# Masks and softmax sums as column-tiled products, and a transpose buffer moved to another PSUM pool, in a recurrent attention kernel

## The chip, the cores and the metric

The kernel runs on one core of a Trainium2 chip. The metric is the device time of one launch in microseconds (us), as the median of several launches.

The engines are named as the profile names them: PE is TensorE's matrix products, PEld its loads of the stationary operand, DVE is VectorE, ACT is ScalarE, POOL is GpSimd. An *eviction* is the copy of a product's result from its PSUM buffer to the buffer that later work reads. A *turn* is VectorE's transpose of a projection in 32x32 blocks (`STREAM_TRANSPOSE`); a cast follows it.

## The reference, cut to what matters

Four layers run one after the other: A, B, A, B. Layer A is a segmented attention that this change doesn't touch. Layer B is recurrent: 64 segments of 32 tokens, each with 8 memory rows in front, and the memory of a segment is the output of the one before. So the 64 steps are a chain, and nothing of one step's queries can start before the last step's output.

```
def _B_ref(x, mem0, Wq, Wk, Wv, Wo, seg_len):      # D = 640, H = 32 heads, Dh = 128, M = 8
    mem = mem0
    for s in range(n_seg):                         # 64 steps
        h = jnp.concatenate([mem, xs], axis=1)     # 40 rows
        q, k, v = (einsum('btd,dhe->bhte', h, W) for W in (Wq, Wk, Wv))
        scores = einsum('bhqe,bhke->bhqk', q, k) * scale
        scores = where(mask, scores, -1e9)
        p = softmax(scores)
        o = einsum('bhte,hed->btd', einsum('bhqk,bhke->bhqe', p, v), Wo)
        mem = o[:, :M, :]
    ...
x = x + _A_ref(_layernorm(x), ...); x = x + _B_ref(_layernorm(x), ...)   # and both once more
```

## The kernel before

A step of layer B works on two halves of 16 heads, b = 0 and 1. Its projections are *column-tiled*: four products with 32 stationary columns each sit side by side in the 128x128 array and write to the four groups of 32 partitions (`tile_position=(0, 32 * j)`), which the profile shows as `128*32`. Scores and output projection have this form too (half of the score products use only 8 of the 32 columns). The mask (an identity times the mask, which starts the accumulation that the scores add to) and the sums (a block matrix of ones times the exponentials) are whole products, `128*128`. The products with the values are row-tiled, `32*128`.

```
def ln_tr(g):                                     # transposes of the layer norm, in the last step of each four
    xn = ln_n.pop(g)
    tps = ps_tile([128, NCH, 128], BF16, "b_lntps")         # pool of 3 PSUM banks, shared with all that follows
    for c in range(NCH):
        nc.tensor.transpose(tps[:, c, :], xn[:, 128 * c:128 * c + 128], C.identb[:])
    ...
def scores(b):
    t = SP[b] = ps_tile([128, 512], F32, "b_SP")
    ...                                            # sp is a view of the first 224 columns of t
    nc.tensor.matmul(sp[:, :, 0:40], lhsT=C.identb[:], rhs=mask..., start=True, stop=False)
    for r in range(4):
        for k, n in ((0, 32), (1, 8)):
            for j in range(4):
                nc.tensor.matmul(o, lhsT=KT..., rhs=QT..., start=False, stop=True, tile_position=(0, 32 * j))
    nc.scalar.activation(out=PT[:, b]..., in_=t[:, 0:224], func=ACT.Exp, ...)

def sums(b):
    ...                                            # 4 products, lhsT = blk[:, k] (128 x 128)

def normalise(b):
    nc.scalar.activation(out=flat, in_=SP[b][:, 256:480], func=ACT.Ln)
    nc.scalar.activation(out=flat, in_=flat, func=ACT.Exp, scale=-1.0)
    nc.vector.tensor_tensor(out=PT[:, b], in0=PT[:, b], in1=R[:], op=ALU.mult)
    ...
# the middle of a step; each qk() is 20 products and a 32x32 turn plus a cast on VectorE
qk(W.wq, "b_Qa", 0, QT); qk(W.wk, "b_Ka", 0, KT)
while late: late.pop(0)()                          # residual add of the last step, 2 x 0.5 us on VectorE
...
qk(W.wq, "b_Qb", 1, QT)
scores(0)
qk(W.wk, "b_Kb", 1, KT)
while xn_pending: ln_tr(xn_pending.pop(0))         # one step in four
sums(0); normalise(0)
VPass(0).run()                                     # 20 products, then evac("dve", Vsb[:, 0, :], ...)
scores(1)
V1 = VPass(1); V1.run(3)
values(0)                                          # the row-tiled products: need PT (normalised) and Vsb
...
V1.run(2)
sums(1)
take("act", 0, 0); take("act", 0, 1)               # evictions of the values, on ScalarE
normalise(1)
...
op.run(4); op.run(4)                               # output projection of the first half
...
```

In the traces each engine starts its work in program order (only TensorE's loads run ahead of its products). The four steps of each group differ a little. I call them kinds 0 to 3: in kinds 0, 1 and 3 the last step's residual add sits between the turns of Ka and Qb on VectorE, kind 2 is without it, and kind 3 has the layer norm's transposes.

## Time and profile before

| | kernel before |
|---|---|
| time | 2560.89 us median of 3 (2560.43 to 2561.15) |
| PE busy | 2346.4 us, 92% of the profiled span of 2552.9 us |
| DVE busy | 1668.9 us, 65% |
| a step of layer B, median of kinds 0, 1, 2, 3 | 13.81, 13.83, 13.94, 14.70 us |

A step is measured in the trace from its first Q product to the next step's. Two layers have 64 steps each; the medians are over the 30 to 32 steps of one kind.

The windows view of the kernel before, one line for most of the first layer B: span, busy time (and count) of PE, PEld, DVE, ACT, POOL, then granted clock, DMA share, GB/s:

```profile
370.00:1252.00 882.00, 862.95 (x23072) 470.08 (x23068) 600.54 (x1289) 250.04 (x737) 372.31 (x842) 1.00 0.09 22
```

PE is busy for 863 of 882 us there, at full clock. It is tempting to read this as "TensorE is the limit, and whatever shortens its work shortens the time". The Trainium skill, "Perfetto Trace Analysis", section "Identifying the Most-Contended Engine", warns that busy time of matmuls is no good measure of how near TensorE is to its limit, because they are pipelined. Here is TensorE in a step of kind 0 (start us, duration us, engine, operation, out<-in, shape, count):

```profile
819.85 1.27 PE L91 MATMUL b_Qb<-b_wq,b_hT 128*32 128x512 bf16 x20
821.04 0.24 PE L91 MATMUL b_SP<-b_mask,c_identb 128*128 128x160 bf16 x1
821.27 0.37 PE L91 MATMUL b_SP<-b_QT,b_KT 128*32 128x40 bf16 x32
821.48 1.28 PE L91 MATMUL b_Kb<-b_wk,b_hT 128*32 128x512 bf16 x20
822.70 0.33 PE L91 MATMUL b_SP<-b_PT,b_blk 128*128 128x160 bf16 x4
822.96 1.26 PE L91 MATMUL b_V<-b_wv,b_hT 128*32 128x512 bf16 x20
824.15 0.24 PE L91 MATMUL b_SP<-b_mask,c_identb 128*128 128x160 bf16 x1
824.33 0.37 PE L91 MATMUL b_SP<-b_QT,b_KT 128*32 128x40 bf16 x32
824.55 0.84 PE L91 MATMUL b_V<-b_wv,b_hT 128*32 128x512 bf16 x12
825.32 0.20 PE L91 MATMUL b_OTL<-b_PT,b_Vsb 32*128 32x40 bf16 x4
```

Read the starts, not the durations: a group's duration runs to the modelled end of its last product, and the next group starts before that. From Qb to the first mask are 1.19 us, though two projections in a row are 1.08 us apart; mask to scores takes 0.18 us or more.

VectorE in the same stretch of the kernel before:

```profile
820.15 0.72 DVE L91 STREAM_TRANSPOSE b_TQ<-b_Ka 128x512 f32<-128x512 f32 x1
820.90 0.23 DVE L91 CAST b_KT<-b_TQ 128x128 bf16<-128x128 f32 x1
821.05 1.00 DVE L91 TENSOR_TENSOR b_XO<-b_OPS,b_XO 64x320 f32<-64x320 f32 x2
822.08 0.72 DVE L91 STREAM_TRANSPOSE b_TQ<-b_Qb 128x512 f32<-128x512 f32 x1
...
823.94 0.61 DVE L91 TENSOR_TENSOR b_PT<-b_PT,b_R 128x224 bf16<-128x224 bf16 x1
824.47 0.68 DVE L91 CAST b_Vsb<-b_V 128x512 bf16<-128x512 f32 x1
```

VectorE works without a pause from the turn of Ka to the eviction of V at 825.15 (824.47 + 0.68), and TensorE's value products start at 825.32. An engine that is busy for 65% of the span has no slack in this half of the step, and TensorE comes only 0.17 us after it.

The transposes of a step of kind 3, TensorE before; the bracket is the idle time before a group and what ended it:

```profile
806.78 1.28 PE L91 MATMUL b_Kb<-b_wk,b_hT 128*32 128x512 bf16 x20
808.14 0.44 PE L91 MATMUL b_lntps<-c_identb,b_xn 128*128 128x128 bf16 x5
808.42 0.32 PE L91 MATMUL b_SP<-b_PT,b_blk 128*128 128x160 bf16 x4
809.03 1.26 PE L91 MATMUL b_V<-b_wv,b_hT 128*32 128x512 bf16 x20 [0.29 <-DVE b_TQ L91]
```

The transposes take a turn in the pool of three banks, so they wait for VectorE's turn of Qb, and V then waits for that of Kb.

### The profile page before, as it was taken

What the parts mean: (1) busy time and instruction counts of PE and PEld (TensorE: products, weight loads), DVE (VectorE), ACT (ScalarE), POOL (GpSimd) and SP (SyncE); (2) the same over time, 40 slices, a digit from 0 to 9 for tenths busy, and PEclk for the clock granted to TensorE, in tenths of its full rate; (3) what the DMA queues carried; (4) which work ended last, traced back from release to release, by engine and by line L of the source; (5) the groups of instructions that cost most, each with busy time, mean ns of one, the idle gap of its engine ahead of it and who ended that gap; (6) DMA issues with size and microseconds to landing.
All of it is one profiled execution on the core that took longest, in us unless ns stands there. A gap on an engine that the chain in (4) does not pass through costs nothing. (4 is left out here: it accounts for less than half of the span.)

```text
span 2552.9 us, 119988 instructions
## 1 busy us (share of the span) xinstructions
PE 2346.4 (92%) x53196; PEld 1266.5 (50%) x53196; DVE 1668.9 (65%) x3771; ACT 921.6 (36%) x2067; POOL 1014.8 (40%) x2333
## 2 busy tenths in 40 slices
PE   6888979999999999999778879699999999999997
PEld 3444435555555555555434445355555555555554
DVE  5666646676666666766556666466766766676665
ACT  4666722222323232222256657132222222222322
POOL 2334434444444444444323334244444444444442
PEclk9988979999999999999989889899999999999999
DMA  6563340001000110000123233400000000000000
GB/s 184 145 173 96 104 133 22 22 22 24 23 22 23 24 23 23 24 20 19 36 88 109 78 105 110 138 20 20 21 20 19 20 19 21 20 19 22 17 16 15
DMA packets 98834, 131.62 MB, mean 52 GB/s; under 512 B 20592, under 2 KB 84096, under 8 KB 96384
## 3 DMA queue, kind: packets, MB, share of 16 engines
q1 hardware_dynamic: 96704, 122.20, 17.4%
q8 instruction: 418, 6.85, 1.1%
q10 hardware_dynamic: 1600, 1.66, 0.2%
q14 instruction: 112, 0.92, 0.1%
HBM read 89.17 MB, written 26.21 MB: 45 GB/s over the span
## 5 line engine op out<-in xcount | busy, mean ns | idle before, releaser
L91 PEld LDWEIGHTS <-b_hT 128*32 128x32 bf16 x15520 | 418.9, 96 | 332.0 <-issue 46.0
L91 ACT ACTIVATE b_PT<-b_SP 128x224 bf16<-128x224 f32 x256 | 91.4, 357 | 871.9 <-PE b_SP L91 871.9
L91 PE MATMUL b_V<-b_wv,b_hT 128*32 128x512 bf16 x5120 | 348.4, 382 | 8.1 <-DVE b_TQ L91 8.1
L91 ACT ACTIVATE a_PT<-a_S 128x768 bf16<-128x768 f32 (+1 forms) x384 | 325.3, 892 | 78.3 <-PE a_S L91 72.7
L91 PE MATMUL b_OPS<-b_wo,b_OTsb 128*32 128x320 bf16 x8192 | 325.3, 300 | 5.4 <-DVE b_OTsb L91 5.3
L91 POOL TENSOR_TENSOR b_Rtot<-b_Rtot,b_R 128x160 bf16<-128x160 bf16 x256 | 158.2, 618 | 306.0 <-ACT b_R L91 306.0
L91 POOL CAST b_QT<-b_TQ 128x384 bf16<-128x384 f32 x254 | 140.7, 554 | 328.8 <-DVE b_TQ L91 328.8
L91 DVE CAST b_Vsb<-b_V 128x512 bf16<-128x512 f32 x256 | 175.7, 686 | 119.7 <-PE b_V L91 119.6
L91 PEld LDWEIGHTS <-b_OTsb 128*32 128x32 bf16 x8192 | 195.9, 96 | 100.6 <-DVE b_OTsb L91 50.2
L91 ACT CAST b_OTsb<-b_OTL 128x320 bf16<-128x320 f32 x384 | 150.9, 427 | 226.3 <-PE b_OTL L91 192.0
L91 POOL CAST b_KT<-b_TQ 128x384 bf16<-128x384 f32 x254 | 142.6, 562 | 130.4 <-DVE b_TQ L91 130.4
L91 POOL TENSOR_SCALAR_AFFINE_SELECT a_PT<-a_PT 128x256 bf16<-128x256 bf16 x256 | 109.6, 432 | 211.9 <-ACT a_PT L91 200.3
L91 PE MATMUL b_Qa<-b_wq,b_hT 128*32 128x512 bf16 x2560 | 162.9, 382 | 22.1 <-DVE b_hT L91 19.1
L91 DVE TENSOR_TENSOR b_PT<-b_PT,b_R 128x224 bf16<-128x224 bf16 x256 | 118.6, 463 | 79.0 <-ACT b_R L91 76.3
L91 PE MATMUL b_Ka<-b_wk,b_hT 128*32 128x512 bf16 x2560 | 164.6, 383 | 0.0
L91 PE MATMUL b_Kb<-b_wk,b_hT 128*32 128x512 bf16 x2560 | 164.3, 380 | 0.0
L91 PE MATMUL b_Qb<-b_wq,b_hT 128*32 128x512 bf16 x2560 | 163.0, 380 | 0.0
L91 PE MATMUL a_PP<-a_xnT,a_wt 128*128 128x512 bf16 x560 | 155.2, 413 | 2.3 <-DVE a_t1k L91 0.9
L91 PE MATMUL a_S<-a_qk 32*128 32x512 bf16 (+3 forms) x1024 | 142.5, 319 | 7.2 <-ACT a_PT L91 6.0
L91 DVE STREAM_TRANSPOSE b_TQ<-b_Qa 128x512 f32<-128x512 f32 x128 | 91.8, 717 | 80.2 <-PE b_Qa L91 36.3
L91 DVE STREAM_TRANSPOSE b_TM<-b_OPS 128x320 f32<-128x320 f32 x126 | 65.1, 517 | 115.2 <-PE b_OPS L91 115.2
L91 DVE CAST a_qk<-a_PP 128x512 bf16<-128x512 f32 x128 | 88.0, 688 | 70.0 <-PE a_PP L91 70.0
(161 smaller groups left out, 3946.8 us busy)
## 6 DMA issues: line engine op xcount, KB each, us to landing
a_wt<-a_wpad SPq DMA_DIRECT2D x112, 160.0 KB
b_wo<-in_B_Wo_dram SPq DMA_DIRECT2D x8, 1280.0 KB
b_Vt<-b_Vtb SPq DMA_DIRECT2D x512, 16.0 KB
b_XO<-xres SPq DMA_DIRECT2D x256, 30.0 KB
a_wvo<-in_A_wo_dram SPq DMA_DIRECT2D x8, 800.0 KB
b_wq<-in_B_Wq_dram SPq DMA_DIRECT2D x20, 256.0 KB
b_wk<-in_B_Wk_dram SPq DMA_DIRECT2D x20, 256.0 KB
xres<-a_xo SPq DMA_DIRECT2D x16, 320.0 KB
```

The costliest lines, as they stand in the source:

```text
L91: r = f(*a, **k)
```

## The change

The intent is to keep TensorE in one tile mode from the projections through masks, scores and sums. The Trainium skill, "TensorEngine Tiling (Array Packing)", section "Key Properties", says that a change of tiling mode drains the engine. The mask and the sums become four products of 32 columns each. The transposes (still 128x128) move to the pool of the value products, so that the pool of three banks turns without them.

```
-            tps = ps_tile([128, NCH, 128], BF16, "b_lntps")
+            tps = pot.tile([128, NCH, 128], BF16, name="b_lntps", tag="ot")
...
-                nc.tensor.matmul(sp[:, :, 0:40], lhsT=C.identb[:], rhs=mask[:].unsqueeze(1).to_broadcast([128, 4, 40]),
-                                 start=True, stop=False, skip_group_check=True)
+                for j in range(4):
+                    nc.tensor.matmul(sp[32 * j:32 * j + 32, :, 0:40], lhsT=C.identb[:, 32 * j:32 * j + 32],
+                                     rhs=mask[:].unsqueeze(1).to_broadcast([128, 4, 40]),
+                                     start=True, stop=False, tile_position=(0, 32 * j), skip_group_check=True)
...  (sums)
                 for k in range(2):
-                    lhsT = blk[:, k].rearrange("p j n -> p (j n)")
-                    ... two products
+                    for part in range(2):
+                        for j in range(4):
+                            c0, c1 = ((16, 56), (40, 56))[k] if part == 0 else (0, 16)
+                            rhs = PT[:, b, :, 0:16] if k else PT[:, b, :, 40:56] if part else PT[:, b, :, 16:56]
+                            nc.tensor.matmul(sm_[32 * j:32 * j + 32, :, c0:c1], lhsT=blk[:, k, j],
+                                             rhs=rhs, start=(k == 0 and part == 0), stop=(k == 1),
+                                             tile_position=(0, 32 * j), skip_group_check=True)
```

A step has 30 products and 30 loads more: 6 for the masks, 24 for the sums.

More of the change, by code (lines that the diff above doesn't have):

```diff
@@ L974, in sums @@
                 for k in range(2):
-                    lhsT = blk[:, k].rearrange("p j n -> p (j n)")
-                    first, last_ = (k == 0), (k == 1)
-                    nc.tensor.matmul(sm_[:, :, 40 * k:56] if k else sm_[:, :, 16:56], lhsT=lhsT,
-                                     rhs=PT[:, b, :, 0:16] if k else PT[:, b, :, 16:56],
-                                     start=first, stop=last_, skip_group_check=True)
-                    nc.tensor.matmul(sm_[:, :, 0:16], lhsT=lhsT, rhs=PT[:, b, :, 0:16] if k else PT[:, b, :, 40:56],
-                                     start=False, stop=last_, skip_group_check=True)
+                    for part in range(2):
[5 more added lines that the diff above has]
+                                             tile_position=(0, 32 * j), skip_group_check=True)
             def normalise(b):
```

## The prediction

> **What bounds the kernel.** TensorE: the page has PE busy 92% of the span, 98% in the two B stretches (370 to 1255 us, 1635 to 2552 us, windows view), with the clock at 1.00 and 0.99. A B step lasts about 13.8 us (14.7 in the fourth of each four, which has the layer norm's transposes), 128 steps in all. But PE busy is not PE needed: the timeline shows a loop through VectorE in every step, and at several points PE arrives only just before its operand.
>
> **What the change removes (TensorE starts, timeline).** A 20-product projection followed by another takes 1.076 us; followed by the mask product it takes 1.197, followed by the sums 1.217. Mask to first score takes 0.175 us, though 160 columns stream in about 0.07. So each change between 128x128 and 128x32 products costs about 0.11 to 0.14 us. This fits the Trainium skill, "TensorEngine Tiling (Array Packing)", Key Properties: changing the tiling mode drains the engine. The change makes mask and sums 128x32 like their neighbours. Six of the ten or so switches per step go; those around the value products (32x128) stay. The four tiles of one product should overlap: mask 0.24 -> about 0.07 us, sums 0.26 -> about 0.15 us, in spite of 30 more products and loads per step. Sum over a step: about 1.0 us of TensorE issue time, 128 us (5%) over 128 steps. That is the ceiling.
>
> **How much is on the critical path.** Little, I think:
> - scores(0): its first product starts 0.146 us after VectorE's K cast ends in nearly every step, the same delay as the next step's first Q product after its operand. It already waits for VectorE. Mask(0)'s 0.28 us gains about 0.
> - From K to the values(0) products VectorE runs back to back in steps 0 and 1 of four (turns, casts, residual add 1.0 us, normalise 0.6, V eviction 0.69). values(0) starts 0.17 us after the V eviction; the shortest seen is 0.057. Gain 0.03 to 0.11 us.
> - Step 2 (no residual add in the way): slack 0.26, and the normalise follows the sums. Gain 0.13 to 0.25.
> - Step 3: the transposes now take a buffer of the value pair pool. Today they start 0.053 us after VectorE's Qb turn (waiting for its buffer), and the V projection waits 0.29 us for the Kb turn. Both waits go, although the transposes (still 128x128) now cost two switches of their own. ScalarE's copy (0.69 us) stays in front of the logarithm. Gain 0.35 to 0.5.
> - Second half: the output product starts 0.155 us after ScalarE's first value eviction (shortest 0.053). Gain 0.01 to 0.1 per step.
> Sum over four steps 0.6 to 1.35 us, times 32: 20 to 43 us.
>
> **Prediction: 2529 us (-1.2%)**, 8 in 10 between 2510 and 2548. Faster by over 2%: 0.10; within 2%: 0.89; slower: 0.01.
>
> **What would show it.** Mask products about 4x256, start of mask to scores set by the K cast, still 0.146 after it; Kb to sums 1.08 (no layer norm); first V to mask 1.08; mask(1) to scores(1) about 0.07; new PE waits <-DVE b_Vsb and <-ACT b_OTsb of about 0.1 to 0.3 us; transposes no longer behind the Qb turn; the steps shortened by about 0.1, 0.1, 0.3, 0.5 us. Layer A unchanged. VectorE's, ScalarE's and GpSimd's order is unchanged.
>
> **What would make it wrong.** (1) The 0.146 at scores(0) includes a drain, so that the first half gains more; (2) four column tiles don't overlap in the mask or sums, which then cost more; (3) the value pair pool, with two buffers, makes values(0) wait for ScalarE's copy of the transposes; (4) VectorE's normalise (0.39 to 0.61 us, longer when GpSimd runs) shifts against GpSimd's casts.

## More of the kernel before

From the profile page of the kernel before, the line of busy times and the queue that brings instructions:

```profile
PE 2346.4 (92%) x53196; PEld 1266.5 (50%) x53196; DVE 1668.9 (65%) x3771; ACT 921.6 (36%) x2067; POOL 1014.8 (40%) x2333
...
q8 instruction: 418, 6.85, 1.1%
```

## The result, and the profile after

| | before | after |
|---|---|---|
| time | 2561.02 us (2560.43 to 2561.37, 4 runs) | 2529.07 us (2527.88 to 2531.68, 4 runs) |
| ratio | | 0.9877, interval 0.986 to 0.9894: 1.2% faster |
| step, kinds 0 to 3 | 13.81, 13.83, 13.94, 14.70 us | 13.61, 13.62, 13.63, 14.14 us |
| first Q product to scores(0), kinds 0 to 2 | 3.585 us | 3.585 us |
| first Q product to values(0), kinds 0 to 3 | 7.63, 7.63, 7.63, 8.41 us | 7.52, 7.52, 7.43, 7.95 us |
| values(0) after the V eviction's end, kinds 0 to 3 | 0.175, 0.174, 0.264, 0.361 us | 0.057 us in all |
| output product after the first value eviction's end | 0.155 to 0.168 us | 0.052 us in all |

The figures of the steps are medians, worked out from the starts and ends of the instructions in the trace.

The page after:

```profile
PE 2293.3 (91%) x57036; PEld 1304.1 (52%) x57036; DVE 1670.4 (66%) x3771; ACT 913.0 (36%) x2067; POOL 1017.6 (40%) x2333
...
q8 instruction: 448, 7.34, 1.2%
```

The windows view after, first layer B:

```profile
370.00:1243.00 873.00, 840.98 (x25002) 490.73 (x24994) 603.29 (x1291) 246.12 (x738) 373.88 (x843) 1.00 0.10 23
```

The windows start at slightly different points of the layer, so compare shares: TensorE was busy for 97.8% of its stretch (862.95 of 882) and is for 96.3% (840.98 of 873). Some of what TensorE gained, it now waits. The first layer's steps themselves went from 886.5 to 874.0 us. The timeline of TensorE after, in the same step of kind 0:

```profile
818.36 1.27 PE L91 MATMUL b_Qb<-b_wq,b_hT 128*32 128x512 bf16 x20
819.44 0.26 PE L91 MATMUL b_SP<-b_mask,c_identb 128*32 128x160 bf16 x4
819.79 0.37 PE L91 MATMUL b_SP<-b_QT,b_KT 128*32 128x40 bf16 x32
819.99 1.28 PE L91 MATMUL b_Kb<-b_wk,b_hT 128*32 128x512 bf16 x20
821.07 0.36 PE L91 MATMUL b_SP<-b_PT,b_blk 128*32 128x160 bf16 x16
821.36 1.26 PE L91 MATMUL b_V<-b_wv,b_hT 128*32 128x512 bf16 x20
822.44 0.26 PE L91 MATMUL b_SP<-b_mask,c_identb 128*32 128x160 bf16 x4
822.51 0.39 PE L91 MATMUL b_SP<-b_QT,b_KT 128*32 128x40 bf16 x32
822.74 0.84 PE L91 MATMUL b_V<-b_wv,b_hT 128*32 128x512 bf16 x12
823.72 0.20 PE L91 MATMUL b_OTL<-b_PT,b_Vsb 32*128 32x40 bf16 x4
```

Every projection of this step is now followed after 1.08 us: the switches from projections to masks and sums are gone. That the 0.12 to 0.14 us came with the change of mode and not with the longer load of 128 stationary columns can be seen inside the whole products of the kernel before: its four sums products, each with such a load, start 0.080, 0.028 and 0.029 us apart (medians). The second mask takes 0.07 us to its first score (822.44 to 822.51), so its four tiles overlap, as the Trainium skill has it for tiles ("TensorE: Matmul & The Clock Gate", section "Measured speedup vs the span model": about 4 ns for each tile more). Here the tiles start 17, 2 and 4 ns apart. But the first mask, which starts 0.11 us earlier against Qb, is followed by a wait of 0.35 us: Qb to scores is 1.43 us after and 1.42 before. And from the V products to the value products (822.74 to 823.72) it takes 0.98 us where it took 0.77.

VectorE after, the end of the same stretch:

```profile
819.56 1.00 DVE L91 TENSOR_TENSOR b_XO<-b_OPS,b_XO 64x320 f32<-64x320 f32 x2
820.59 0.72 DVE L91 STREAM_TRANSPOSE b_TQ<-b_Qb 128x512 f32<-128x512 f32 x1
...
822.99 0.68 DVE L91 CAST b_Vsb<-b_V 128x512 bf16<-128x512 f32 x1
```

The eviction ends at 823.67, and the value products start at 823.72. VectorE's stretch, from the turn of Ka to that end, takes as long as before (5.00 us before and 5.01 after). The V products now start at 821.36, 0.05 us after the turn of Qb (820.59 + 0.72), and it is that turn that they wait for: they need a buffer of the pool of three. In the view of waits, the line of loads waiting for the V eviction before:

```profile
PEld L91 <- DVE b_Vsb L91: 54.5, 128, 0.6
```

and after (us in total, times, longest):

```profile
PEld L91 <- DVE b_Vsb L91: 80.1, 128, 0.7
```

The sum has grown, but the name alone proves little: the line counts 128 waits in the kernel before too, where a control below (x_vact_b) shows that nothing is lost to this eviction. An experiment has to decide.

Step of kind 3 after:

```profile
805.86 1.28 PE L91 MATMUL b_Kb<-b_wk,b_hT 128*32 128x512 bf16 x20
807.07 0.45 PE L91 MATMUL b_lntps<-c_identb,b_xn 128*128 128x128 bf16 x5
807.45 0.34 PE L91 MATMUL b_SP<-b_PT,b_blk 128*32 128x160 bf16 x16
807.62 1.25 PE L91 MATMUL b_V<-b_wv,b_hT 128*32 128x512 bf16 x20
```

Kb to V is 1.76 us in place of 2.25. The transposes start before the turn of Qb ends, and V no longer waits.

### The profile page after: what moved, and what is told of

Its sections match the earlier page's. It is cut to its first block, busy times and chain, and to the rows that moved or that the text cites. A ratio compares the mean times of both kernels' runs of the same rounds, so it can differ in the third digit from the quotient of the medians.

```text
span 2527.8 us, 127670 instructions
## 1 busy us (share of the span) xinstructions
PE 2293.3 (91%) x57036; PEld 1304.1 (52%) x57036; DVE 1670.4 (66%) x3771; ACT 913.0 (36%) x2067; POOL 1017.6 (40%) x2333
## 5 line engine op out<-in xcount | busy, mean ns | idle before, releaser
L91 PEld LDWEIGHTS <-b_hT 128*32 128x32 bf16 x15520 | 424.9, 96 | 322.6 <-issue 41.7
L91 DVE TENSOR_TENSOR b_PT<-b_PT,b_R 128x224 bf16<-128x224 bf16 x256 | 126.3, 493 | 59.9 <-ACT b_R L91 59.3
```

Of the source, the lines that this page charges most:

```text
L91: r = f(*a, **k)
```

## The experiments

Theory A, mine: the operand waits decide. TensorE's gain comes through only up to the next operand that another engine delivers (K cast at scores(0), V eviction at values(0), first value eviction at the output product). Theory B, the rival: the removed switches and the overlapped products pay wherever they stand, TensorE being the limit. A third question came with the trace after, see "Stalls" below. Twelve runs were made, eleven of new kernels and one of the changed kernel again; all gave correct results. Each was timed in five rounds. The kernel before had medians of 2560.7, 2561.4 and 2560.3 us in the three sets, so the times below can be compared within 1 us or so.

| kernel | us, median (range) | ratio to before | steps of kinds 0 to 3, us | stalls: us (count) |
|---|---|---|---|---|
| before | 2560.7 | 1 | 13.81 13.83 13.94 14.70 | 0.7 (2) |
| x_ln: transposes moved only | 2550.2 (2545.2 to 2552.5) | 0.9955 | 13.81 13.83 13.94 14.26 | 1.0 (3) |
| x_mask: masks tiled only | 2541.5 (2539.0 to 2544.1) | 0.9924 | 13.69 13.72 13.73 14.50 | 0.4 (1) |
| x_sums: sums tiled only | 2543.5 (2540.9 to 2545.9) | 0.9935 | 13.61 13.62 13.64 14.59 | 10.0 (20) |
| after | 2529.1 (2527.9 to 2531.7) | 0.9877 | 13.61 13.62 13.63 14.14 | 8.5 (18) |
| after_again | 2530.1 (2527.6 to 2535.3) | 0.9887 | 13.64 13.61 13.63 14.14 | 10.2 (23) |
| x_mask0: after, first mask whole | 2533.3 (2530.7 to 2536.6) | 0.9895 | 13.59 13.62 13.64 14.14 | 12.2 (26) |
| y_nomask: after, both masks whole | 2529.0 (2527.0 to 2531.4) | 0.9880 | 13.58 13.62 13.63 14.14 | 7.6 (19) |
| y_lean: y_nomask, 12 sums products | 2523.9 (2520.4 to 2529.5) | 0.9853 | 13.58 13.62 13.63 14.13 | 7.0 (17) |
| y_pad: after, first mask issued 3 times | 2528.0 (2524.7 to 2531.0) | 0.9869 | 13.58 13.62 13.63 14.14 | 10.5 (23) |
| x_vact: after, V eviction on ScalarE | 2504.8 (2503.6 to 2508.4) | 0.9789 | 13.39 13.41 13.41 13.89 | 9.5 (23) |
| x_vact_b: before, V eviction on ScalarE | 2559.9 (2553.6 to 2563.3) | 0.9996 | 13.81 13.83 13.93 14.71 | 0.9 (3) |
| v_nomask: y_nomask, V eviction on ScalarE | 2527.5 (2524.1 to 2529.7) | 0.9867 | 13.59 13.62 13.62 14.10 | 8.7 (22) |
| y_best | 2510.1 (2506.1 to 2514.3) | 0.9802 | 13.56 13.59 13.42 13.89 | 6.2 (15) |

Stalls are counted in the profiled run of each kernel, in the B layers: single spacings between two products in a row that are over 0.22 us longer than the median spacing at the same place of the same kind of step.

### One part at a time

x_ln has only the line of the transposes' buffer of the diff above.

> Only the transposes move to the value pair pool; mask and sums stay 128x128. Theory A (the gain is what the operand waits leave): only the fourth step of each four changes, as its transposes no longer wait for the Qb turn and the V projection no longer waits for the Kb turn; values(0) comes 0.4 to 0.5 us earlier there, until the V eviction binds: 30 such steps, 12 to 15 us faster, other steps unchanged at 13.81, 13.83, 13.94 us. Theory B (what the changed kernel gains is the removed tile mode switches, wherever they stand): nearly nothing here, within 3 us of before.

Measured: 10.5 us faster. Only kind 3 moved, by 0.44 us (14.70 to 14.26, which makes 13 us over 30 steps), with values(0) 0.058 us after the V eviction. Theory A holds; B falls as far as it says that only switches pay. This part removes none.

x_mask has only the four tiled mask products.

> Only the two mask products per step are column-tiled. Theory A: mask(0) is worth 0 (scores(0) still start 0.146 us after the K cast, Q to scores(0) still 3.585 us); mask(1) takes 0.22 us off TensorE before values(0), of which the V eviction lets through 0.115, 0.115, 0.21 and 0.22 us in the four kinds of step: 18 to 23 us faster. Theory B (each removed switch and each overlapped product pays): 2 x 0.28 us x 128 = 70 us faster.

Measured: 19.3 us faster; steps shorter by 0.12, 0.11, 0.20 and 0.21 us; first Q product to scores(0) 3.584 to 3.585 us as ever. So the second mask pays and the first does not, and the second pays up to the V eviction: values(0) come 0.058 us after it in kinds 0 to 2. B's 70 us are far off.

x_sums has only the tiled sums.

> Only the sums are column-tiled. Theory A: first half 0.11, 0.11, 0.25 and 0 us per kind of step (limited by the turn of Qb, the V eviction, the turn of Kb), second half 0.1 us each (limited by the first value eviction): 0.9 us over four steps, 25 to 30 us faster, less a few us if TensorE's instruction stream stalls more (30 more products and loads per step minus none). The three parts alone then sum to about 60 us, double what they save together (32 us), because they share the same slack. Theory B: parts add up to the joint gain; x_ln + x_mask + x_sums = 32 us.

Measured: 17.2 us faster, where 25 to 30 were expected. The steps did what theory A said (0.20, 0.21, 0.30, 0.11 us shorter; over 126 steps some 26 us), but 20 stalls took about 10 us. The three parts alone sum to 10.5 + 19.3 + 17.2 = 47 us, 15 more than the 32 of all together: they draw on the same slack. It is less than the "double" expected: that set a sum of the parts without stalls beside a joint gain that has stalls in it. By the medians of the steps alone the parts make 13.2 + 20.0 + 25.8 = 59.0 us, and all together 39.8. (The 30 products of the expectation are those of the whole change; the sums add 24.) In kinds 0 to 2 x_sums is already as short as the whole change.

### Is the first mask worth anything, is any mask?

```
 def scores(b):  # x_mask0
+    if b == 0: one whole product, as before
+    else:      four tiled products
```

> The changed kernel, but with the first mask of each step whole (128x128) again, the second tiled. Theory A: scores(0) wait for the K cast, so this costs nothing: within 4 us of the changed kernel (2525 to 2533 us), and scores(0) still 0.146 us after the K cast. Theory B (a switch costs wherever it stands): 0.28 us x 128 = 36 us slower than the changed kernel, 2565 us.

Measured: 2533.3 us, 0.3 us beyond what theory A allowed and 32 us from B. Medians of the steps are those of the changed kernel; the 4 us are within what the stalls vary (12.2 us in place of 8.5).

y_nomask has `scores` of the kernel before, the rest of the changed kernel.

> The changed kernel with both masks whole (128x128) again: transposes in the pair pool and tiled sums only, 12 TensorE instructions fewer per step. Theory A: the V eviction binds anyway once the sums are tiled, so the mask's tiling is worth nothing more in the pair: steps' medians as in the changed kernel (13.61, 13.62, 13.63, 14.14), time within 5 us of it, though the mask alone was worth 19 us. Theory B: 19 us slower, as the part alone gained 19.

Measured: 2529.0 us, the changed kernel's time. An edit that is worth 19 us alone is worth nothing beside the other two. The reason is to be seen at values(0): with the sums tiled, TensorE reaches them no later than the V eviction lets them start. In kinds 0 and 1 it is a tie. Values(0) come 0.777 us after the second V group, which is TensorE's own pace, and 0.062 us after the eviction, where 0.057 is the usual delay; in kinds 2 and 3 TensorE waits some 0.015 and 0.045 us. So that the second mask is worth exactly nothing here is a coincidence of two lengths: had TensorE's path been longer, part of it would have paid, as in x_mask.

### Take VectorE out of the way

```
-                        evac("dve", Vsb[:, self.b, :], self.ps[:])
+                        evac("act" if self.b == 0 else "dve", Vsb[:, self.b, :], self.ps[:])
```

> The changed kernel with the first V eviction of each step on ScalarE instead of VectorE. Theory A (in the changed kernel values(0) wait for VectorE's backlog, ending in that eviction): values(0) come when TensorE arrives, from Q to values(0) about 7.30, 7.30, 7.17 and 7.6 us in place of 7.52, 7.52, 7.43 and 7.95: 25 to 33 us faster by the steps' medians, around 2500 us, less what more stalls of TensorE's instruction stream take back. Theory B (TensorE bounds the changed kernel, VectorE's queue is no matter): no change, within 4 us of 2529.

Measured: 2504.8 us, 24 us faster than the changed kernel and 2.1% faster than before (the interval of the ratio, 0.9775 to 0.9803, lies on both sides of the 2% mark). First Q product to values(0) is 7.31, 7.31, 7.21 and 7.71 us, as theory A had it but for kind 3 (7.6 expected). TensorE of x_vact in a step of kind 0:

```profile
812.49 1.26 PE L91 MATMUL b_V<-b_wv,b_hT 128*32 128x512 bf16 x20
813.56 0.26 PE L91 MATMUL b_SP<-b_mask,c_identb 128*32 128x160 bf16 x4
813.63 0.39 PE L91 MATMUL b_SP<-b_QT,b_KT 128*32 128x40 bf16 x32
813.86 0.84 PE L91 MATMUL b_V<-b_wv,b_hT 128*32 128x512 bf16 x12
814.64 0.20 PE L91 MATMUL b_OTL<-b_PT,b_Vsb 32*128 32x40 bf16 x4
```

The value products come 0.78 us after the second V group, the time that the products between need in the kernel before as well. The wait of 0.2 us is gone.

The same edit in the kernel before is the control:

> The kernel before with the first V eviction of each step on ScalarE. Theory A: in the kernel before, TensorE with its mode switches arrives at values(0) later than that eviction in every kind of step (0.17 to 0.36 us after it), so this changes nothing: within 4 us of 2561, steps' medians 13.81, 13.83, 13.94, 14.70. The same edit took 24 us off the changed kernel. Theory B (the edit relieves VectorE, which helps in both): about 24 us here too.

Measured: 0.9996, interval 0.9982 to 1.001. No change, in any kind of step. So in the kernel before TensorE was the later one at values(0), in the changed kernel VectorE is. Theory B's reading of it falls. The edit also lightens VectorE's load, which alone is worth nothing here.

Then the mask again, with the eviction out of the way:

> The changed kernel with both masks whole again AND the first V eviction on ScalarE. Theory A: with the eviction out of the way TensorE's own path binds, and the second mask's tiling, worth nothing before, now is worth its whole 0.22 us per step: 22 to 30 us slower than x_vact, 2525 to 2533 us, Q to values(0) about 7.52 us again. Theory B (the mask's tiling is worthless in the pair, as y_nomask had it): 2505 us.

Measured: 2527.5 us, and 7.52 us to values(0) again in kinds 0 and 1. With the transposes moved and the sums tiled in all four, the two edits make this table (us):

| | V eviction on VectorE | on ScalarE |
|---|---|---|
| masks whole | 2529.0 | 2527.5 |
| masks tiled | 2529.1 | 2504.8 |

Each edit alone is worth 0 to 1.5 us, both together 24 us. That is what a wait for the later of two paths looks like: shortening one only uncovers the other.

### Stalls

In the trace after, medians of the steps say 39.8 us less over the 126 steps of the B layers (sum of each step's median), but the steps themselves sum to only 31.0 us less (1773.2 to 1742.3 us). About 9 us come back in single steps. Several of the longer ones are of this form, TensorE of the changed kernel in a step of kind 0:

```profile
437.50 0.18 PE L91 MATMUL b_OTL<-b_PT,b_Vsb 32*128 32x40 bf16 x4
...
438.32 0.20 PE L91 MATMUL b_OTL<-b_PT,b_Vsb 32*128 32x40 bf16 x4 [0.62 <-issue]
```

The operands of these products were there (their group had begun at 437.39), and still TensorE sits for 0.8 us in the middle. If all records of TensorE's queue (products, loads and semaphore instructions) are counted through the trace, 16 of the 18 such stalls fall on number 193 or 194 of each 256; in x_sums 18 of 20 fall on 163 or 164 in the first layer and on 132 or 133 in the second. (That trace lacks 62 product records, about half of them before each of these layers, so there too it is about number 194.) The queue of instructions (q8 of the page) moved 418 packets before and 448 after: 7,680 products and loads more came in 30 packets more, 256 to a packet. So the stalls recur once per packet of TensorE's instructions, most likely where one ends and the next begins; the count can't show where in a packet the number 193 lies. Theory C was that more instructions mean more of them. Two kernels test it. In y_lean masks are whole, and the last two sums products of each tile are one that reads its operand twice:

```
+    both = bass.AP(tensor=flat.tensor, offset=flat.offset, ap=[flat.ap[0], [56, 4], [40, 2], [1, 16]])   # columns 0:16 and 40:56
+    outs = (sm_[:, :, 16:56], sm_[:, :, 0:16], both)
+    rhss = (PT[:, b, :, 16:56], PT[:, b, :, 40:56], PT[:, b, :, 0:16].unsqueeze(2).to_broadcast([128, 4, 2, 16]))
```

> As y_nomask, and the last two of the four sums products per tile made one (rhs read twice): 28 TensorE instructions fewer per step than the changed kernel. Theory C (part of the expected gain goes to stalls of TensorE's instruction stream at every 256th instruction, which come when instructions are consumed too densely): medians of the steps unchanged, the stalls (10.7 us over the medians in the changed kernel's profile) fall to 3 to 8 us, time 2519 to 2527 us. Against it: stalls are random, the time stays at 2529 or rises.

Measured: 2523.9 us by the median, but the range (2520.4 to 2529.5) touches that of y_nomask, the intervals of the ratios overlap, and in its profiled run (2529.5, its slowest) the steps exceeded their medians by 12.5 us, not by 3 to 8. Inconclusive.

y_pad issues the first mask's products three times:

> The changed kernel with the four tiled products of the first mask issued three times (same result: each starts the group anew), 16 more TensorE instructions per step, in the 0.28 us in which TensorE waits for the K cast there. Theory C: medians of the steps unchanged within 0.03 us, but more stalls at every 256th instruction: excess over the medians 14 to 25 us in place of 10.7, time 2533 to 2545 us. Against it: only waiting time is filled, nothing changes, 2529 within 3 us.

Measured: 2528.0 us, 11.9 us over the medians. Theory C fails in this form: 16 more instructions per step in a waiting stretch change nothing. What fits all runs is density: in the first layer B before, none of the 176 stretches of 256 such records, cut at the number where the stalls fall, was issued in less than 3.3 us (the shortest took 3.39); after, 28 of 189 were, and the kernels without tiled sums (before, x_ln, x_mask, x_vact_b) have 0.4 to 1.0 us of stalls, those with them 6.2 to 12.2. The tiled sums put 24 more products and loads between the second projections and the value products than whole ones. No run varied density alone, and the fit is loose (of the 28 dense stretches 6 are followed by a stall, and 7 of that layer's 13 stalls at the usual number follow a stretch that took longer), so that stays a reading of the traces.

> The changed kernel once more. 2525 to 2533 us. If TensorE's stalls at every 256th instruction come from the program alone, a second trace has them in the same steps; if from a race with other transfers, in other steps, with a similar sum of 8 to 14 us over the medians.

Measured: 2530.1 us, 11.8 us over the medians, and the stalls again at number 193 or 194 in all but two cases. In the first layer six steps stall in both traces (4, 12, 20, 23, 28 and 43), others in one only. So the place is the program's, and the length is partly chance. How the next packet comes to be late, none of these runs shows.

### A further version

y_best is x_vact with the first mask whole, y_lean's sums, and the residual add after the turn of Qb, so that the V projection gets its buffer earlier.

> x_vact, with the first mask whole, sums in three products per tile, and the residual add after the turn of Qb in place of before it (so that the V projection doesn't wait for that turn behind 1.0 us of adds). Theory A: V starts 0.13 us earlier in the steps 0 and 1 (perhaps 3), 8 to 12 us faster than x_vact, and up to 5 us by fewer stalls: 2490 to 2499 us.

Measured: 2510.1 us, 5 us *slower* than x_vact, where 6 to 15 faster was expected. The intervals of the two ratios overlap (0.9788 to 0.9816, and 0.9775 to 0.9803), but the steps of kinds 0 and 1 are clearly longer, 13.56 and 13.59 us in place of 13.39 and 13.41. V no longer waits for the turn of Qb: it starts 0.763 us after that turn in kinds 0 and 1, in x_vact 0.053 us after it. But VectorE's order now has the add in front of the turn of Kb. TensorE of y_best, kind 0:

```profile
813.85 0.28 PE L91 MATMUL b_SP<-b_mask,c_identb 128*32 128x160 bf16 x4
814.25 0.37 PE L91 MATMUL b_SP<-b_QT,b_KT 128*32 128x40 bf16 x32
```

and VectorE of y_best:

```profile
812.18 1.00 DVE L91 TENSOR_TENSOR b_XO<-b_OPS,b_XO 64x320 f32<-64x320 f32 x2
813.22 0.72 DVE L91 STREAM_TRANSPOSE b_TQ<-b_Kb 128x512 f32<-128x512 f32 x1
813.97 0.23 DVE L91 CAST b_KT<-b_TQ 128x128 bf16<-128x128 f32 x1
```

The K cast of the second half ends at 814.20, and scores(1), which read it, start at 814.25, 0.4 us after their mask. I had looked at the buffer that the add delays and not at the operand. Of all kernels, x_vact is the fastest: 2504.8 us.

## Why the prediction was right or wrong

The time (2529 us predicted, 2529.07 measured) and the class were right. That the middle was hit to the microsecond is luck: two terms were off and cancelled.

- **The ceiling is not the gain**: right. TensorE's issue time per switch and overlap was as costed: projection to mask 1.199 to 1.079 us, projection to sums 1.217 to 1.076, mask(1) to scores 0.175 to 0.07 (0.115 in kind 2), sums to the next product 0.26 to 0.155 where nothing is waited for. Of the 128 us ceiling, a quarter came through.
- **scores(0) gain nothing**: right. They start 0.146 us after the K cast before and after; x_mask0 confirms it. Why 0.146 and not the 0.05 seen elsewhere can be read from the trace: these scores wait for VectorE and for GpSimd, and a separate semaphore instruction stands in TensorE's queue for one of the two. It starts 0.04 us after the cast, the load of K 0.076 us after it, and the first score 0.031 us after the load. Second-half scores and value products have no such instruction.
- **The V eviction binds values(0)**: right for the changed kernel, and shown by x_vact against x_vact_b.
- **The transposes**: right. "Both waits go" held, and x_ln gives 0.44 us per step of kind 3 for the 0.35 to 0.5 predicted.
- **How much slack is used**: in the sum "0.6 to 1.35 us over four steps, times 32" the right end was true: 0.20 + 0.21 + 0.30 + 0.56 = 1.28 us by the medians. The low end assumed that a product could follow its operand by no less than the 0.146 us seen at scores(0). The runs show 0.057 after the V eviction and 0.052 after the value eviction, in nearly every step: the 0.146 belongs to the wait with the extra instruction. The worry (1) that scores(0) would gain was unfounded.
- **What was missing**: one wait, and the stalls, about 9 us. The wait: in kinds 0 and 1 the V projection now waits for the turn of Qb. Between Kb and V the tiled sums save 0.25 us in kind 2 (1.477 to 1.232), but in kinds 0 and 1 only 0.11 (1.477 to 1.367). The list of what could go wrong has the tiles not overlapping, the pool and VectorE's normalise, but not the supply of TensorE's instructions, though the change adds 60 per step, 48 of them for the sums. Worry (4) came true in small: the normalise of kind 0 takes 0.69 us after, 0.61 before.

The prediction's signs for the profile held but for one: the output product's wait for ScalarE's eviction can be read from the trace (0.052 us after its end), but the views name it only for 0.2 us of a single step. Its guess for the steps (0.1, 0.1, 0.3 and 0.5 us shorter) was low in kinds 0 and 1, where it was 0.20 and 0.21.

## What to carry to other kernels

When an engine is busy for 98% of a stretch, still ask at each operand how long after its arrival the product starts, and compare with the shortest delay seen at the same kind of wait: in this kernel the difference was the most that a faster TensorE gained there. Where two paths end within a fraction of a microsecond of each other, shortening one is worth that fraction, and the pair of edits (here tiled mask and an eviction on an idle engine) is worth far more than the sum of each alone, so test them together. Parts that share slack don't add up either: one of the three parts of this change could be taken out again at no cost.

## What the Trainium skill lacked or had wrong

- "TensorEngine Tiling (Array Packing)", Key Properties, says that a mode switch drains the engine but not what it costs. Here a switch from column-tiled to whole products costs 0.12 us (projection to mask, 1.199 to 1.079 us) or 0.14 (projection to sums, 1.217 to 1.076), and one back to tiled products 0.1 us (mask to scores, 0.175 to 0.07 us with the same 160 columns). These are differences between the two kernels' medians.
- "Runtime: NRT & Kernel Launch", Instruction fetch mechanics, treats the blocks in which instructions come, but gives no length for a stall at one. Here stalls of 0.25 to 1.04 us recur at one number of each 256 records of TensorE's queue, 8.5 us in all after the change and 0.7 before (that block ends cause them is likely, not shown).
- "TensorE: Matmul & The Clock Gate", section "Wait — 56ns, not 53.3ns?", has a floor of about 25 ns between the starts of products. For products in four column tiles that isn't a bound: 32 score products take 0.206 us, 6.4 ns each. The packing section of the same page, with 4 ns between tiles, agrees better.
- "Perfetto Trace Analysis", Identifying the Most-Contended Engine, is right that matmul busy time misleads. Of the two measures that it gives in its place, the busy share of the loads rose from 50 to 52% while the time fell by 1.2%; the change adds 3,840 loads. It doesn't tell what TensorE waits for, which was the question here. The other, the operations done against the peak, was not worked out.
- No page that I found gives the delay from an operand's end to the product that reads it: 0.052 to 0.057 us after an eviction by ScalarE or VectorE, 0.146 us after the K cast, where a semaphore instruction stands between.
